# A dummy exponential first on ScalarE, the first load of x in two, and a new order of the work

## The chip, the cores and the metric

One core of a Trainium2 chip runs the kernel. Its engines are TensorE (PE in the profile; PEld are its weight loads), VectorE (DVE), ScalarE (ACT), GpSimd (POOL) and SyncE (SP); 16 DMA engines move data between HBM and SBUF. The metric is the device time of one execution in microseconds (us); lower is better. Beside it stands the span, from the first to the last instruction of the program as the profiler records it.

## The reference

A causal depthwise convolution of 7 taps, with one softmaxed set of taps for each of 8 heads of 24 columns, is followed by a token mixer without softmax. Batch 8, 4224 tokens, 192 columns, a hidden width of 64, all float32 outside.

```python
w = softmax(weight, axis=-1)                     # (8 heads, 7 taps)
x = sum over k of w[h, k] * x_pad[b, s + k, h]   # causal, zero-padded by 6
wq, wk = x @ w_q, x @ w_k                        # (B, S, 64)
W_tok = einsum('bsd,btd->bst', wq, wk) / sqrt(64)
mixed = einsum('bst,btd->bsd', W_tok, x)
out = maximum(mixed, 0) @ w_out
```

Since nothing non-linear stands between `W_tok` and `mixed`, the kernel never forms the 4224 x 4224 matrix. It forms the 192 x 192 gram matrix of a batch, G = x^T x, then M = w_k^T G / 8 (64 x 192), and mixed = wq M.

## The kernel before, in words

**Tiling.** A batch's 4224 tokens are cut into 35 chunks of 122 (`CW`), each loaded with the 6 tokens before it, so that a chunk fills 128 partitions. x comes from HBM as float32 and is cast to bf16 by the loading DMA into `XW`, which holds five batches (`NX`). Batch 0 is loaded in four groups of 9, 9, 9 and 8 chunks, the others in two of 18 and 17. Chunk 0, the full chunks and the last chunk of a batch are each a DMA of their own, all issued on POOL's queue.

**Stages of a batch**, with the names that the profile shows:

1. *Convolution* (`conv`, L352 to L354): for each pair of heads and each group, a product of a banded 128 x 128 matrix (`BAND`) with the chunks, into one or two of the eight PSUM banks; drained as bf16 to `Y` by ScalarE or VectorE (`y`, L671).
2. *Transposes* (`tr_lo`, `tr_hi`, L358 to L360 and L728), drained by VectorE to `YTL` and `YTH` (L698, L738).
3. *Gram* (L795), six chunks a time, one bank for all; then a turn of part of it, and the product M (drains `gsb`, `gt`, `msb`, `mbd`).
4. *wq* (L757, L761), drained to `WQT` (L778).
5. *Mix* of the batch before, in five blocks: `mix_lo` (L888) and `mix_hi` (L900, L908) form the mixed tokens, a relu drains them to `RT` (L925, L926), `fin` (L954) and `fin_other` (L972) multiply by `w_out`, drains go to `OUT` (L993), and SP issues the store (L1001). The last batch's stores are halved.

**The start.** SP loads `weight` to all partitions (L366). VectorE writes an identity's ones, zeroes the run-up tile `RUNUP` and other small tiles. POOL cuts `IDENT` out of the ones with `affine_select` (L403). TensorE multiplies zeros from `RUNUP` (the run-up, L378) while nothing else is there to do. From `IDENT` come `STEP`, its transpose `STEPT` (copied by ScalarE, L424), and the 0/1 masks `OTHER` and `OWN` (L428 to L436). The softmax runs in `WEX` (maximum L440, differences L446 and L452, exponential on ScalarE L461, sums, reciprocal, product L466 to L471), gives `TAPS` (L473), and sixteen small products per fill (L353 and L354, "taps,stept") spread the taps into PSUM, from where ScalarE and VectorE copy the bands (L511). The first convolution needs the band, one more run-up (`run_3`) and all DMAs of the first group.

**Order.** Each piece of work is an `Op` with a number in the order of its creation. `PLAN` lists all numbers in the order in which they are placed, with a letter for the engine (P: TensorE in its op's own array shape, F: TensorE in the full 128 x 128 shape, A: ScalarE, D: VectorE, G: POOL, S: SP; a small letter: one drain for two banks) and, for TensorE's first op of a group, its PSUM bank. An engine executes its ops strictly in that order, each after its semaphore waits. The estimated lengths in the code (`ns`, `tail`, `lands`) are not used when the kernel is built. `turns` fixes a minimal order of VectorE's first ops.

**Numbers used below.** In the order before: 14 `IDENT`'s select, 38 chunk 0 and 39 chunks 1 to 8 of the first group, 40 to 43 the other groups of batch 0, 57 to 60 batch 1, and so on. In the order after, one op more from number 23 on (the dummy) and two more from 42 on (the load's second part).

Of the kernel before, what the change touches and what calls it, by code (L numbers as in the profile page):

```python
# [14 lines left out]
39G 0S 2D 14G 1D 9D 5D 6D 7D 15D 20D 21D 4D 38G 40G 44S 41G 42G 43G 57G 58G 59G 60G 16P3 17P2 19A 23D 24D  # L15
25D 22D 26A 27D 28D 29D 30D 18P5 31P4 34P1 37P7 35D 36D 3D 32A 73P0 33A 75P3 10D 11D 76D 77P1 78A 79P7 80D
12D 74A 109P3 135P7 87P0 88A 61G 62G 110D 85F1 86A 83F6 84D 81F0 82A 93F4 94D 13D 89F6 90A 95F5 45S 96A 91F0
111F3 92A 112D 137P 136P 97F2 98D 103F5 104A 99F4 101F3 102D 8D 46S 113F0 114D 119P6 120D 100A 117F5 118D
115F4 116D 139P 121P2 122D 123P1 124D 138P 140P 141D 49A 47A 48A 125P6 126D 133P7 134A 127P3 154P1 155D 156A
51A 151F4 152A 153D 148F6 149A 150D 157F1 158A 159D 131P0 132D 129P5 130D 128A 50A 142F4 143A 176F7 177D  # L20
178F6 179D 202P4 169P0 170D 171D 163P2 54A 52A 53A 144P5 147A 146A 145A 160P6 204P 166P0 161A 162D 244P5
164D 165A 167A 168D 203P 230P6 247D 233A 56A 216P0 219A 180P1 181D 190P7 191D 186P5 187D 215P2 217A 55A 63G
184P6 185D 218D 282P0 182P7 206P 200P2 201D 183D 205P 188P5 189D 285P2 283A 284A 286D 287A 288P0 289A 290A
279P6 280D 281A 207P 194P5 195A 64G 294P2 295A 192P1 193A 208D 209P0 296D 229P6 210D 231D 232A 220P4 224P2
221P 222A 243P0 245A 246A 225P 226D 227D 258P6 261A 223D 228S 65G 66G 309P7 310D 198P4 199A 196P2 272P3 274A
67G 68G 69G 70G 71G 72G 105G 106G 107G 108G 172G 173G 174G 175G 303G 304G 234P0 238P5 271P4 273D 235P 236D
197A 237A 307F7 308D 239F 240D 241A 242S 211F4 213A 257P0 259D 212A 260A 214A 248P2 252P6 275P5 249P 250D
251A 253P 254A 276P 277D 278S 300P0 301A 347P4 291P2 292A 293A 297P5 298A 333P0 255D 256S 302D 413P1 414A
415A 350A 335P 306G 299D 315P3 316D 319P5 320D 346P6 348D 349A 311F1 312D 361F2 364A 419F3 420D 421A 425F6
426D 427A 305G 337P 317P2 321P1 322D 266P4 318D 262P6 313F3 314D 267F 268A 269D 263F 264D 265A 270S 422F1  # L30
423D 424A 375F3 378D 329P4 330A 331P5 332D 334P 416P6 417A 418D 410P1 411A 412D 325P4 326A 327P3 328A 360P6
362D 363A 355P1 351P4 356P 357D 358A 352P 402P6 404D 353D 354A 359S 323P3 324A 389P7 392A 369P1 365P5 370P
371A 372D 374P3 366P 367A 368D 373S 376A 436F7 428F1 429D 430A 431F5 432D 433A 437D 403P3 336P 338P 339D
442P6 443D 446P5 447D 434P2 435D 340P7 405A 377A 379P3 341A 388P0 390A 383P5 342F7 344A 343A 391D 345A 380F
381A 382D 384F 385A 386D 387S 440F0 441D 473P1 475A 476D 397P3 406P5 393P6 398P 399D 400A 407P 408A 409S
394F 543F0 544D 545D 395A 396A 401S 438F4 439D 488P5 555P2 556A 557A 491D 474P6 477A 448P0 444P7 537P1 538A
449D 460P4 445D 540P5 541A 542D 456P3 457A 454P1 455D 502P0 505A 463P 501P6 503D 504A 458P5 552P0 553A 554D
539D 450P3 451A 459A 464P 558P6 559A 560D 546P0 547A 548D 461P 452P5 453D 478P6 487P2 489A 490D 482P0 479F
480D 481A 563F5 564D 483F 484D 485A 486S 492P2 465P 530P7 532A 549F5 550D 551A 493F 494D 495A 561F7 562D
516F1 519A 496P5 515P2 517A 518A 529P0 531A 497P 498D 499D 500S 462P 571P1 572D 569F7 570D 670F2 671D 672D  # L40
466A 467F5 468A 533P4 510P0 506P6 565F5 566D 469F2 472A 471A 470A 534F 535D 536S 567F3 568D 511P 512A 513D
507P 508A 509A 514S 520P4 573P2 575P0 576D 521F 522A 523D 664F6 665A 643F3 646A 667F0 666A 673F4 585P6 586A
674A 574D 581P2 582A 675A 587P3 589P 577P7 578A 668D 669D 601P0 615P6 604D 524P1 600P4 602D 525P 526A 629P7
632D 527A 528S 603A 618D 590P 579P0 580A 583P2 592P 584A 609P4 628P6 630A 631D 605P0 610F 611A 612D 688F2
689D 606P 656P6 607A 608D 613S 614P4 616D 588P 657P7 617A 659A 591P 642P1 623P4 658A 619P6 644A 645A 593D
594F3 595D 624F 625A 626D 620F 621A 622D 627S 679F0 680A 681D 596F2 599A 598A 597A 690F4 691D 637P6 633P0
638F 639D 640A 685F2 686A 687D 676F4 677D 678A 634F 635D 636A 641S 682F6 683D 684A 651P2 647P4 660P1 652P
653D 654A 648P 661P 662D 663S 728P0 731A 742P7 745D 698P6 699D 700P3 701D 649A 650A 655S 702P2 703D 791P0
792A 793A 692P7 693D 797P5 798A 799D 800P3 756P0 759A 801D 794P1 795A 796A 694P5 695D 727P6 696P0 697D 802D
704P3 705D 729A 806P1 807D 808A 712P0 713D 710P6 711A 730A 817P5 818D 815P3 816D 708P1 709A 706P2 707A 732P6  # L50
741P4 743A 744D 736P0 733F 734A 735D 770F2 773A 737F 750P4 783P3 746P6 738A 739D 740S 751P 752A 753A 755P1
757A 758D 785D 747P 748A 714P0 716P 803P4 749A 754S 784P3 924P1 718P 804A 805D 812P6 813D 814D 933P4 934D
935A 786A 719P 717P 715P 720A 925D 926A 769P6 771D 772A 760P4 787P3 764P0 788P 789A 790S 761P 762A 763D 765P
721P2 766D 767A 768S 722A 809P6 810A 841P3 843P 723P5 725A 724A 726A 811D 823P7 824D 819P6 820D 829P2 921P0
830D 821P4 822D 918P5 919D 827P2 828D 825P7 826D 922A 923A 920A 927P0 928A 837P4 855P6 858D 842P 839P7 840D
869P5 872D 929A 838D 835P1 836A 831P0 832D 846P 778P6 774P1 854P4 856D 857A 779P 780A 781A 775P 776D 845P
883P0 886A 777D 782S 844P 847A 930P5 833P4 931A 932D 834A 848P2 849D 944P3 945D 863P0 868P6 859P4 870D 871A
897F2 900A 864F 865A 866D 860F 861A 862D 867S 942F3 943D 896P6 898A 910P2 912D 877P0 899A 873P4 878P 879A
880D 911P3 913A 874P 875D 876A 881S 882P6 884D 885A 850F2 853A 939F0 940D 941A 936F3 937A 938D 852A 851A
914P5 905P6 887P0 906P 907D 908A 891P3 915P 916A 917S 888P 892P 893D 946P2 947D 954P7 956P6 957D 952P5 953D  # L60
948P3 949D 955D 889A 890A 894A 895S 950P0 951D 968P4 982P1 985D 966P2 967A 996P5 999A 958P6 959A 962P7 963A
901P2 981P0 983D 984A 902P 1009P5 903D 904A 909S 1011A 1012D 973P 1010P7 1013A 971P 995P0 997D 998A 986P2
990P5 987P 988D 989A 1024F7 1027A 991P 992A 993D 994S 1004P0 1000P2 1005P 1006A 1007A 1023P6 1001P 1002A
1003D 1008S 1037P5 1039D 1025A 1026D 972P 969P 970P 974D 1038P2 1040A 960P0 961D 1018P5 1014P2 975F4 976D
# [11 lines left out]
class Op:  # L76


    n = 0
# [144 lines left out]
def bass_lightweight_conv__then__hypermixer_token_mlp_kernel(  # L224
# [31 lines left out]
    def groups_of(b):  # L256
        size = 9 if b == 0 else 18
        return [list(range(c, min(c + size, NCC))) for c in range(0, NCC, size)]
# [828 lines left out]
```

## Time and profile before

| | us |
|---|---|
| Runs, median (lowest to highest of 3) | 169.34 (169.01 to 169.45) |
| The profiled execution, its own time | 167.91 |
| Its span | 166.2 |
| First convolution begins | 7.59 |
| First / second / third / fourth group of batch 0 landed | 6.66 / 9.52 / 11.82 / 13.83 |
| First half of batches 1, 2, 5, 7 landed | 20.65 / 29.45 / 74.67 / 110.17 |
| Second half of batches 1, 2, 7 landed | 24.90 / 33.96 / 114.38 |
| Last product of TensorE ends | 160.27 |
| Last drain ends | 161.33 |
| Last store lands | 165.62 |

The landings are the times of issue plus the times to landing in the trace. A few of the page's groups, for the cost of a drain on either engine (line, engine, operation, tiles, count | busy us, mean ns of one | idle before):

```profile
L671 ACT CAST y<-ps 122x432 bf16<-122x432 f32 (+2 forms) x71 | 33.7, 519 | 10.9 <-PE ps L354 9.4
L993 DVE COPY out_sb<-ps 128x384 f32<-128x384 f32 (+1 forms) x64 | 32.9, 540 | 6.1 <-PE ps L972 4.6
L993 ACT COPY out_sb<-ps 128x384 f32<-128x384 f32 (+1 forms) x72 | 31.4, 479 | 8.8 <-PE ps L972 8.2
L671 DVE CAST y<-ps 122x408 bf16<-122x408 f32 (+2 forms) x57 | 31.6, 587 | 5.4 <-PE ps L354 3.1
```

The mean is an instruction's length from its own start; where two overlap, the busy time counts the overlap once.

### The profile page before, as it was taken

The numbers are of one execution on the slowest core, as the hardware profiler recorded it, in microseconds if no ns is written. First come the engines' busy times: TensorE is split into PE (matmuls) and PEld (weight loads), VectorE is DVE, ScalarE is ACT, GpSimd is POOL, SyncE is SP. The second block draws the span as 40 slices with busy tenths as digits, with TensorE's granted clock in tenths as the row PEclk, the third lists the DMA queues.
The fourth block names the chain that finished last, engine by engine and source line by source line (L and its number), as shares of the span: only waits on it lengthen the run. The fifth ranks groups of instructions, "written<-read, shape, count | busy, mean of one in ns | idle before, by whom it ended". The sixth has DMA issues, their size and how long they took to land.

```text
span 166.2 us, 6578 instructions
## 1 busy us (share of the span) xinstructions
PE 155.5 (94%) x2852; PEld 115.2 (69%) x2852; DVE 132.6 (80%) x276; ACT 117.3 (71%) x285; POOL 30.4 (18%) x39
## 2 busy tenths in 40 slices
PE   6969999999999999999999999998999999999940
PEld 2448758777777687787767777687888867785620
DVE  5566889879799799898967889966698889879960
ACT  1446186699958978868587788894856895969920
POOL 7999653535400200000000000000000000000000
PEclk9999999999999999999999999999999999999997
DMA  2999999999999999999999999999330595478996
GB/s 20 175 191 185 205 191 196 189 194 195 301 322 238 285 290 282 316 263 191 296 287 283 285 281 302 324 250 343 142 127 4 196 365 219 186 287 323 376 366 234
DMA packets 48156, 40.33 MB, mean 243 GB/s; under 512 B 37632, under 2 KB 40960, under 8 KB 48128
## 3 DMA queue, kind: packets, MB, share of 16 engines
q0 software_dynamic: 36128, 13.61, 68.6%
q1 hardware_dynamic: 12000, 26.31, 43.9%
q8 instruction: 22, 0.36, 0.8%
q14 instruction: 6, 0.05, 0.1%
HBM read 27.56 MB, written 25.95 MB: 322 GB/s over the span
## 4 chain that ended last, share of the span: by engine, by line
PE 79%; DMA 8%; POOL 4%; ACT 3%; issue 2%; DVE 0%; another core or an unknown queue 0%; DVEq 0%; POOLq 0%
PE ps L795 13%; PE ps L954 12%; PE ps L972 10%; DMA xw<-in_x_dram 8%; PE ps L353 6%; PE ps L888 5%; PE ps L757 5%; PE ps L358 4%; PE ps L352 4%; PE ps L728 4%; PE ps L761 4%; PE ps L908 3%; PE ps L359 3%; POOL xw L556 3%; PE ps L354 3%
## 5 line engine op out<-in xcount | busy, mean ns | idle before, releaser
L925 ACT ACTIVATE rt<-ps 128x512 bf16<-128x512 f32 (+1 forms) x70 | 37.6, 559 | 5.8 <-PE ps L888 3.7
L671 ACT CAST y<-ps 122x432 bf16<-122x432 f32 (+2 forms) x71 | 33.7, 519 | 10.9 <-PE ps L354 9.4
L993 DVE COPY out_sb<-ps 128x384 f32<-128x384 f32 (+1 forms) x64 | 32.9, 540 | 6.1 <-PE ps L972 4.6
L993 ACT COPY out_sb<-ps 128x384 f32<-128x384 f32 (+1 forms) x72 | 31.4, 479 | 8.8 <-PE ps L972 8.2
L671 DVE CAST y<-ps 122x408 bf16<-122x408 f32 (+2 forms) x57 | 31.6, 587 | 5.4 <-PE ps L354 3.1
L556 POOL DMA_DIRECT2D xw<-in_x_dram x34 | 29.9, 892 | 24.8 <-issue 17.4
L795 PEld LDWEIGHTS ps<-y 122*64 122x64 bf16 x840 | 29.0, 111 | 4.0 <-issue 1.2
L795 PE MATMUL ps<-y 122*64 122x64 bf16 (+2 forms) x840 | 31.6, 221 | 0.1
L926 DVE TENSOR_SCALAR rt<-ps 128x512 bf16<-128x512 f32 (+1 forms) x42 | 26.0, 628 | 6.9 <-PE ps L888 5.3
L698 DVE COPY ytl<-ps 128x976 bf16<-128x976 bf16 (+1 forms) x40 | 23.2, 588 | 3.5 <-PE ps L360 2.6
L972 PE MATMUL ps<-wol,rt 64*128 64x192 bf16 (+1 forms) x264 | 25.1, 248 | 0.2
L954 PE MATMUL ps<-woh,rt 64*128 64x192 bf16 x264 | 22.9, 248 | 0.7 <-ACT rt L925 0.4
L353 PE MATMUL ps<-xw,band 128*64 128x432 bf16 (+2 forms) x82 | 19.0, 332 | 0.6 <-DMA xw<-in_x_dram 0.6
L354 PE MATMUL ps<-xw,band 128*64 128x432 bf16 (+2 forms) x82 | 19.1, 334 | 0.0
L972 PEld LDWEIGHTS ps<-wol,rt 64*128 64x128 bf16 (+1 forms) x264 | 15.9, 114 | 4.4 <-PE ps L954 1.0
L778 ACT CAST wqt<-ps 128x512 bf16<-128x512 f32 (+1 forms) x26 | 13.6, 546 | 6.5 <-PE ps L761 6.3
L954 PEld LDWEIGHTS ps<-woh,rt 64*128 64x128 bf16 x264 | 12.5, 113 | 7.9 <-issue 1.4
L954 PE MATMUL ps<-wol,rt 64*128 64x192 bf16 x175 | 15.4, 243 | 0.0
L761 PE MATMUL ps<-yth,wqh 128*64 128x512 bf16 (+1 forms) x72 | 14.8, 361 | 0.0
L757 PE MATMUL ps<-ytl,wql 128*64 128x512 bf16 (+1 forms) x72 | 14.7, 367 | 0.0
L888 PE MATMUL ps<-wqt,msb 64*128 64x512 bf16 (+1 forms) x72 | 13.8, 363 | 0.0
L738 DVE COPY yth<-ps 128x732 bf16<-128x732 bf16 x24 | 12.1, 530 | 0.5 <-PE ps L728 0.5
(116 smaller groups left out, 207.4 us busy)
## 6 DMA issues: line engine op xcount, KB each, us to landing
out_dram<-out_sb SPq DMA_DIRECT2D x28, 768.0 KB, 7.2
xw<-in_x_dram POOLq DMA_DIRECT2D x7, 816.0 KB, 36.2
xw<-in_x_dram POOLq DMA_DIRECT2D x7, 768.0 KB, 38.6
out_dram<-out_sb SPq DMA_DIRECT2D x8, 384.0 KB, 3.9
xw<-in_x_dram POOLq DMA_DIRECT2D x2, 432.0 KB, 6.9
out_dram<-out_sb SPq DMA_DIRECT2D x8, 96.0 KB, 4.9
xw<-in_x_dram POOLq DMA_DIRECT2D x1, 384.0 KB, 5.1
xw<-in_x_dram POOLq DMA_DIRECT2D x8, 45.8 KB, 23.7
```

The source lines that it names most:

```text
L353: e.matmul(out[0:64], lhsT[:, 0:64], rhs, **k)
L354: return e.matmul(out[64:128], lhsT[:, 64:128], rhs, **k)
L556: lambda e, op, part=part: e.dma_start(*part),
L671: return e.copy(dst, src) if op.engine == "ACT" else e.tensor_copy(dst, src)
L698: lambda e, op: e.tensor_copy(YTL[:, b % NYT, t0:t1], bank(mm_l.bank).bitcast(BF16)[:, 0:cols]),
L757: last = e.matmul(ps[64 * i : 64 * i + DH, 0:n], WQL[:, :], YTL[:, b % NYT, starts[i] : starts[i] + n], start=True, stop=False)
L795: mm = e.matmul(bank(where.bank)[p : p + 64, o : o + z - r], Y[0:w, yb, c, r : r + 64], Y[0:w, yb, c, r:z], start=st, stop=end, skip_group ...
L925: return e.activation(dst, src(), AF.Relu)
L926: return e.tensor_scalar(dst, src(), 0.0, None, op0=ALU.max)
L954: last = e.matmul(bank(op.bank + a)[:, (i - q) * D : (i - q) * D + D], RT[p, slot, a if lo else 2, i:n:nt], WOL[p, :] if lo else WOH[p, :] ...
L972: last = e.matmul(bank(fh.bank + a)[:, (i - q) * D : (i - q) * D + D], RT[p, slot, a, i:n:nt], WOL[p, :], start=False, stop=True, skip_gro ...
L993: return e.copy(dst, src) if op.engine == "ACT" else e.tensor_copy(dst, src)
```

## The change

- ScalarE's first instruction becomes a dummy: `Exp` of one column of `RUNUP` into a new tile `EARLY`, which nobody reads. It needs the run-up tile alone; STEPT's copy comes after it.
- The main load of the first group (chunks 1 to 8) is split into chunks 1 to 3 and chunks 4 to 8. Only the first part may go before `IDENT`'s select.
- VectorE's minimal order puts the zeroing of `STEPT`, `WQH`, `WKT` and `WKB` before `STEP`, `OWN` before the maximum, and the zeroing of the last columns of `WQT` behind the second difference.
- The second run-up has 5 products instead of 6.
- Two estimates change (`tail`, `ident`'s length), which the built program doesn't contain.
- `PLAN` is another order: engines of drains, array shapes, banks and sequence. The first convolutions now stand as follows on TensorE: all four of the first group, three of the second, a gram, a transpose, the fourth of the second group; before it was the first group, a transpose, a gram, then the second group. ScalarE has 296 ops instead of 284, VectorE 265 instead of 276, POOL 36 instead of 35.

```diff
 PLAN = """
-39G 0S 2D 14G 1D 9D 5D 6D 7D 15D 20D 21D 4D 38G 40G 44S 41G 42G 43G 57G 58G 59G 60G 16P3 17P2 19A 23D 24D
-25D 22D 26A 27D 28D 29D 30D 18P5 31P4 34P1 37P7 35D 36D 3D 32A 73P0 33A 75P3 10D 11D 76D 77P1 78A 79P7 80D
+40G 2D 1D 9D 5D 6D 7D 4D 14G 41G 39G 42G 43G 44G 45G 59G 60G 61G 62G 63G 64G 23A 10D 11D 12D 15D 20D 21D 22D
+0S 24D 25D 26D 3D 27A 28D 16P6 17P3 18P2 29D 30D 31D 19A 32P0 35P2 33A 38P4 36D 37D 75F5 76D 34A 77P0 78A
...
-        size = 9 if b == 0 else 18
-        return [list(range(c, min(c + size, NCC))) for c in range(0, NCC, size)]
+        cuts = [0,9,18,27,NCC] if b == 0 else [0, 18, NCC]
+        return [list(range(c, z)) for c, z in zip(cuts, cuts[1:])]
...
+    EARLY = sbuf("early", [128, 1], F32)
...
-        tail=3500,
+        tail=3200,
...
-        1800,
+        1160,
...
-    run_2 = run_up(6, after=[turned])
+    run_2 = run_up(5, after=[turned])
...
+    early = add("ACT", lambda e, op: e.activation(EARLY[:, :], RUNUP[:, 0:1], AF.Exp), 1600, needs=[zero_r], vt=-9, kind="early")
+    stept.after.append(early)
...
-    turns = [one, zero_r, zero_x, eps, zero_e, zero_x0[0], step, by_tap, other, zero_s, mx, sub, mine, own, sm, rc, wn, taps, *bands[2:]]
-    turns += [zero_w, zero_q, *zero_k, zero_m, zero_x0[1]]
+    turns = [one, zero_r, zero_x, eps, zero_e, zero_x0[0], zero_s, zero_q, *zero_k, step, by_tap, other, own]
+    turns += [mx, sub, mine, zero_w, sm, rc, wn, taps, *bands[2:], zero_m, zero_x0[1]]
...
-        n = len(full)
-        parts.append(
-            (
-                XW[:, b % NX, full[0] : full[0] + n, :],
-                bass.AP(x_t, base + (CW * full[0] - KC + 1) * D, [[D, 128], [CW * D, n], [1, D]]),
-            )
-        )
+        for c, z in ((1, 4), (4, cs[-1] + 1)) if (b, gi) == (0, 0) else ((full[0], full[-1] + 1),):
+            parts.append(
+                (
+                    XW[:, b % NX, c:z, :],
+                    bass.AP(x_t, base + (CW * c - KC + 1) * D, [[D, 128], [CW * D, z - c], [1, D]]),
+                )
+            )
...
-            first = (b, gi) == (0, 0) and part[0].shape[1] > 1 and len(part[0].shape) == 3
+            first = (b, gi, k) == (0, 0, 1)
```

## The prediction

> **What bounds the kernel now.** I read the page's busy times first, then its row of DMA shares.
>
> ```profile
> PE 155.5 (94%) x2852; PEld 115.2 (69%) x2852; DVE 132.6 (80%) x276; ACT 117.3 (71%) x285; POOL 30.4 (18%) x39
> DMA  2999999999999999999999999999330595478996
> ```
>
> TensorE works 94% of the span. The 16 DMA engines are full from the second to the 28th of 40 slices, and again in the last ones. So three things can set a moment: TensorE's own work, a load of x that it waits for, and, at the end, the stores. The chain of waits says where the loads do (columns: start, length, what).
>
> ```profile
> 7.27 13.38 DMA xw<-in_x_dram
> 20.69 0.37 PE ps L353
> ...
> 113.87 0.51 another core or an unknown queue
> 114.42 0.36 PE ps L353
> ```
>
> The chain leaves TensorE twice for x: the first half of batch 1 lands at 20.65 (7.27 + 13.38) and TensorE starts on it at 20.69; the second half of batch 7 lands at 114.38 and TensorE, idle since 113.87, starts at 114.42. Everywhere else after 10 us it has work: 148.2 us busy in the 150 us from 10 to 160. Then the timeline of the start.
>
> ```profile
> 1.33 1.01 POOL L556 DMA_DIRECT2D xw<-in_x_dram  x1 [0.81 <-POOLq L1072]
> ...
> 2.77 0.20 DVE L412 COPY step<-ident 128x128 bf16<-128x128 bf16 x1 [0.57 <-POOL ident L403]
> ...
> 3.47 2.74 PE L378 MATMUL ps<-runup 128*128 128x512 bf16 x6
> 3.63 1.28 ACT L424 ACT_TABLE_LOAD   x1 [3.63 <-PE ps L360]
> ...
> 4.24 0.22 DVE L452 TENSOR_TENSOR wex<-wex,other 128x56 f32<-128x56 f32 x1
> ...
> 5.00 0.30 ACT L461 ACTIVATE wex<-wex 128x112 f32<-128x112 f32 x1
> ...
> 6.09 0.29 DVE L473 TENSOR_TENSOR taps<-own,wtap 128x128 bf16<-128x128 f32 x1
> ...
> 8.17 0.17 DVE L385 MEMSET wqt<- 64x128 uint32 x1
> ...
> 8.73 1.12 DVE L671 CAST y<-ps 122x432 bf16<-122x432 f32 x2
> ...
> 9.97 0.11 PEld L359 LDWEIGHTS ps<-ident,y 122*64 122x64 bf16 x1 [1.51 <-ACT y L671]
> ```
>
> ScalarE loads its table at 3.63, only when the first matrix to copy is there, so the softmax exponential starts at 5.00 although its operand is complete at 4.46 (4.24 + 0.22). The taps follow at 6.09. Later VectorE clears three small tiles (0.17 at 8.17, then two of 0.11) ahead of its first drains of y (8.73), and TensorE's transposes wait for those until 9.97, 1.5 us. Last, the DMA side: the issue of the load of chunks 9 to 17 (KB, us to landing) and three windows (length; busy us of PE, PEld, DVE, ACT, POOL; clock; DMA share; GB/s).
>
> ```profile
> xw<-in_x_dram POOLq DMA_DIRECT2D x1, 432.0 KB, 6.3
> ```
>
> ```profile
> 5.00:6.00 1.00, 1.00 (x3) 0.15 (x1) 0.60 (x3) 0.30 (x2) 1.00 (x2) 1.00 1.59 189
> 6.00:7.00 1.00, 0.77 (x26) 0.56 (x27) 0.35 (x2) 0.00 (x0) 1.00 (x3) 1.00 1.30 131
> ...
> 162.00:164.00 2.00, 0.00 (x0) 0.00 (x0) 0.00 (x0) 0.00 (x0) 0.00 (x0) 0.96 1.03 363
> ```
>
> That load is issued at 3.24 and lands at 9.52. The share falls to 1.30 between 6 and 7, where the first two loads are through and this one's rows come slowly: a bubble of about 0.3 us of full flow (131 GB/s against 188). In the last stretch the stores keep the engines at a share of 1.03, after TensorE has nothing left.
>
> **Part by part.** All against the profiled execution, 167.91 us with a span of 166.2; the runs have a median of 169.34 (169.01 to 169.45), 1.43 above it, so I subtract the same difference from both.
>
> *Dummy exponential.* It waits for the run-up tile alone (written by 1.34), so the table load of 1.28 is over at about 2.6 and the dummy itself (0.30, the row of the real one, at most) at 2.9; all that is queued behind it on ScalarE waits for later things. The real one then starts when its operand is there: 4.46 instead of 5.00, about 0.5 earlier. STEPT's copy goes behind it (0.18, over at about 5.0), hidden since its reader comes after the taps. The exponential, four VectorE steps and taps keep their lengths: taps end at 5.9 instead of 6.38. *One run-up less* is needed for that: six took 2.74 from 3.47, to 6.2; five (0.43 each) end at 5.8. With six the fills would wait 0.3. The fills then fall wholly into the time when TensorE still runs slowly (run-up matmuls of 512 columns take 0.43, later ones of 512 columns 0.22), some 0.2 more for the two. The first convolution so moves from 7.59 to 7.2 or 7.3.
>
> *Tiles zeroed elsewhere.* The clearing of STEPT, WQH and WKT/WKB (0.16 + 3 x 0.11 = 0.49) moves into VectorE's idle 0.57 before 2.77; OWN (0.38) ahead of the weight's landing at 3.72, where it just fits; WQT (0.17) into the wait for the exponential. VectorE's drains of the first y's come about 0.9 us earlier (0.5 from the taps, 0.4 from the clearing that stood before them).
>
> *Where that leads.* In the new order TensorE does not go on to these transposes: three convolutions of the second load stand ahead, and what is queued behind them (gram, transposes, VectorE's copies of these) waits with them. So its gap ends not at 9.97 but when that load lands, 9.52 + d, d being the shift of the loads. Convolution, gram and transpose fill the time to the third and fourth landing (11.82 + d, 13.83 + d). The fourth group's convolutions started at 14.80, with one gram of 0.50 done that the new order puts later: like for like 14.30 against 13.85 + d, a gain of 0.45 to 0.5 less d. At batch 1 the new order has a turn and, net, one more product for WQ ahead (0.34 + 0.44 in the chain for two half-sums of each kind, about 0.5 for one pair), which uses that up: TensorE arrives near 20.5 + d and waits no longer than now. So **0.48 - d**.
>
> *The load in two* costs one more issue on POOL. The rows are 0.59 for 122 rows, 1.01 for 1024, 1.00 for 1152: 384 and 640 rows cost about 0.7 and 0.85. The first part ends at 2.1 instead of 2.34, IDENT's select follows 0.25 earlier, then 640 rows, chunk 0 (0.57), and the second group is issued at 3.85, not 3.24: 0.6 later, and every later load with it. How much of it reaches the landings, the trace doesn't show. Lower bound: the first rows flow 0.3 earlier as the first issue is shorter, and the bubble closes: d = -0.3. Upper: the second group's rows come 3.0 us after its issue as now, and everything behind is 0.6 later. Between, as the queue holds two loads ahead while they wait: **d = 0.2**. So -0.28, from -0.78 to +0.12.
>
> *The order.* Both orders hold 470 turns of TensorE with 101 and 104 changes between its array shapes, too little to price. I compared what stands ahead of the first use of each load. For the last (second half of batch 7) the new order has three grams (0.50 each), a MIX_LO and a convolution (0.3 to 0.4 each) more ahead, 2.1 us. TensorE arrives near 115.7, after the landing at 114.38, and the wait of 0.51 goes: **-0.5** (0 if order costs it elsewhere). For the others the difference is within 1.7 us and the present slack holds, the tightest being batch 5 (landed 74.67, used 75.57).
>
> *VectorE to ScalarE.* ScalarE has 296 turns for 284, VectorE 265 for 276. By the page, a drain of y is 0.475 on ScalarE (33.7 / 71) and 0.554 on VectorE (31.6 / 57), one of out_sb 0.436 and 0.514, a relu 0.537 and 0.619. Seven y and eight out_sb go over, four relus come back: 0.55 + 0.62 - 0.33 = 0.85 less in all, 0.4 per engine. TensorE hides half or more of it: **-0.2**, from -0.85 to the loss of the ScalarE rival.
>
> *The tail.* From the store issued at 150.33 to the end the queue stays full: 4.9 MB at about 370 GB/s, 13 us, to 164.4. So the end hangs on when this store goes out, not on TensorE's last product. In the new order two FIN groups of the last batch (eight products 0.33; with four, half) stand before it: **+0.33**, from 0 to 0.5. The last drains are four in a row on ScalarE (1.74), against two on VectorE (1.02) now; they hide behind the stores by some 0.5, and without that cover cost 0.7.
>
> Sum: -0.28 - 0.5 - 0.2 + 0.33 = **-0.65**: 167.26 for the profiled execution, **168.7** for the runs.
>
> **Rivals.** *The feed is late by more.* The four clearings now run while POOL writes the 640 rows' descriptors. If they hold it up by their full 0.49, d is 0.6 + 0.49 = 1.1 and the sum +0.25: 169.6. Against it: the first issue ran beside a clearing of 0.46 (VectorE at 1.50) and took 1.01, no more than 1.00 later without one. [...] The row just given speaks against it for this clearing, so I give this rival little.
>
> *ScalarE becomes the bound* (the slower side). Between the turns of the sixth and seventh gram (94.6 and 117.9) ScalarE now has 44 drains and is busy 18.9 of 23.3 us, 9.04 of 10 from 100 to 110; the new order gives it 49 there, 2.4 us more at 0.48. If its idle time there can't be used, TensorE's banks come free late, by 2.4 at most; with half, and without the relief, -0.65 + 0.2 + 1.2: 170.1. From 0.45 lost upwards the kernel is slower than now. For it: VectorE, at 9.68 in the same 10 us, can't help. Against: 4.4 us of idle.
>
> *The drains gain in full.* With 0.85 taken and d = -0.3 the sum is -1.8: 167.5 to 168.1.
>
> *The table load doesn't move, or comes twice*: then the start stays, 1.28 more in the second case, most of it hidden by the wait for the second load; -0.65 + 0.28: 169.0. The single load now serves copy and exponential, so this is unlikely.
>
> **Chances.** Below 0.3% (0.51 us) a measurement here can't be told from no change. Forecast 0.50, spread 168.2 to 169.2 (0.35 faster, 0.15 same); late feed 0.12 (same 0.09, slower 0.03); ScalarE 0.20 (slower); full gain 0.15 (faster); table 0.03 (same). Faster 0.50, same 0.27, slower 0.23. The range, 167.6 to 170.2, leaves out the outer parts of the ScalarE and full-gain cases.
>
> **What would show it.** Table load near 1.4, exponential near 4.5, taps over by 5.9: right at the start. The second group's landing gives d. No wait on the load at 114 and a first use after 115: the second term. A store run of 13 us that starts later against TensorE's work: the tail. It is wrong if the waits move to drains on ScalarE between 95 and 118, or if the loads land over 0.7 later.

## The result and the profile after

| | before | after |
|---|---|---|
| Runs taken together, median (lowest to highest) | 169.39 (169.01 to 169.82), 4 runs | 171.3 (171.15 to 172.24), 4 runs |
| Ratio, 95% interval | | 1.0131 (1.0085 to 1.0177) |
| Profiled execution, its own time | 167.91 | 171.15 |
| Its span | 166.2 | 169.4 |
| Weight landed / real exponential begins | 3.72 / 5.00 | 4.22 / 4.99 |
| First convolution begins | 7.59 | 7.93 |
| Groups 1 to 4 of batch 0 landed | 6.66 / 9.52 / 11.82 / 13.83 | 7.89 / 11.82 / 14.10 / 16.13 |
| First / second half of batch 1 landed | 20.65 / 24.90 | 22.41 / 26.93 |
| Last product of TensorE ends | 160.27 | 162.85 |
| From there to the end of the span | 5.88 | 6.57 |

The change makes the kernel 1.3% slower, some 2.2 us by the ratio (1.9 by the medians). First the page of after: the busy times, and two rows of 40 slices.

```profile
PE 154.7 (91%) x2803; PEld 116.7 (69%) x2811; DVE 127.4 (75%) x265; ACT 122.6 (72%) x297; POOL 31.1 (18%) x40
...
PEclk9996999999999999999999999999999999999996
DMA  3999999999999999999999999998250585478996
```

TensorE is busy 0.8 us less than before while the span is 3.2 us longer: the time went into idling, not into more work. PEclk falls to 6 in the fourth slice (12.7 to 16.9 us), where before it was full. The chain of waits (start, length, what) leaves TensorE early and once more:

```profile
0.70 0.62 issue
1.32 0.89 POOL xw L560
2.61 1.41 POOL xw L560 x2
4.02 7.80 DMA xw<-in_x_dram
...
33.80 0.86 issue
```

From the start to 11.82 nothing but loads of x stands on the chain: the issues on POOL, then 7.80 us from the second group's issue to its landing. The pieces at 20.69 and 114.42, where the chain of before waited for batches 1 and 7, are gone. New is an "issue" of 0.86, in which TensorE waits for nothing that the profile shows. The timeline of the start:

```profile
0.80 1.28 ACT L441 ACT_TABLE_LOAD   x1 [0.80 <-PEq L1076]
...
1.32 0.89 POOL L560 DMA_DIRECT2D xw<-in_x_dram  x1 [0.81 <-POOLq L1076]
...
2.10 0.20 ACT L441 ACTIVATE early<-runup 128x1 f32<-128x1 bf16 x1
...
2.54 11.56 POOL L560 DMA_DIRECT2D xw<-in_x_dram  x13
...
4.24 0.21 DVE L444 TENSOR_REDUCE wmx<-wt_f 128x8 f32<-128x56 f32 x1 [0.72 <-DMA wt_f<-in_weight_dram]
...
4.74 0.22 DVE L456 TENSOR_TENSOR wex<-wex,other 128x56 f32<-128x56 f32 x1
...
4.99 0.30 ACT L465 ACTIVATE wex<-wex 128x112 f32<-128x112 f32 x1 [2.69 <-DVE wex L456]
...
6.07 0.29 DVE L477 TENSOR_TENSOR taps<-own,wtap 128x128 bf16<-128x128 f32 x1
...
7.93 0.36 PE L353 MATMUL ps<-xw,band 128*128 128x216 bf16 x2 [0.50 <-DMA xw<-in_x_dram]
...
11.87 0.28 PE L354 MATMUL ps<-xw,band 128*64 128x216 bf16 x1 [2.67 <-DMA xw<-in_x_dram]
```

The table load stands at 0.80, even ahead of the dummy's wait for the run-up tile, and the dummy is through at 2.30. But VectorE's first step on the weight waits for it until 4.24, so that the real exponential begins at 4.99 as before. The first convolution waits 0.50 for x, and then TensorE idles 2.67 us, to 11.87, for the second group. That group's issue (KB, us to landing; the latter was 6.3), and windows (length; busy us of PE, PEld, DVE, ACT, POOL; clock; DMA share; GB/s):

```profile
xw<-in_x_dram POOLq DMA_DIRECT2D x1, 432.0 KB, 7.8
```

```profile
4.00:5.00 1.00, 1.00 (x4) 0.32 (x3) 0.65 (x3) 0.01 (x1) 1.00 (x2) 1.00 0.77 69
5.00:6.00 1.00, 0.78 (x2) 0.00 (x0) 0.78 (x4) 0.35 (x2) 1.00 (x2) 1.00 1.11 115
6.00:7.00 1.00, 0.58 (x32) 0.58 (x32) 0.33 (x2) 0.10 (x1) 1.00 (x2) 1.00 1.41 164
7.00:8.00 1.00, 0.50 (x10) 0.17 (x4) 0.75 (x2) 0.55 (x2) 1.00 (x3) 1.00 1.05 103
8.00:9.00 1.00, 1.00 (x12) 0.44 (x12) 0.61 (x1) 0.36 (x1) 1.00 (x2) 1.00 1.07 123
12.00:14.00 2.00, 2.00 (x46) 2.00 (x44) 0.61 (x1) 0.94 (x2) 2.00 (x2) 0.66 1.59 191
14.00:16.00 2.00, 2.00 (x17) 1.55 (x13) 1.70 (x3) 0.15 (x1) 2.00 (x4) 0.50 1.57 187
165.00:167.00 2.00, 0.00 (x0) 0.00 (x0) 0.00 (x0) 0.00 (x0) 0.00 (x0) 0.81 1.03 372
```

From 4 to 9 us the DMA engines move 69 to 164 GB/s, where the kernel before had 182 to 189, and 131 from 6 to 7. From 12 on they are full again (191). Behind the idle 2.67 us TensorE's clock is at half (0.50 from 14 to 16). In the last row the stores run at 372 GB/s with TensorE through, as before.

### The profile page after: what moved, and what is told of

Read it like the earlier page. It is cut to its first block, busy times and chain, and to the rows that moved or that the text cites. A ratio compares the mean times of both kernels' runs of the same rounds, so it can differ in the third digit from the quotient of the medians.

```text
span 169.4 us, 6485 instructions
## 1 busy us (share of the span) xinstructions
PE 154.7 (91%) x2803; PEld 116.7 (69%) x2811; DVE 127.4 (75%) x265; ACT 122.6 (72%) x297; POOL 31.1 (18%) x40
## 4 chain that ended last, share of the span: by engine, by line
PE 81%; ACT 6%; DMA 5%; issue 2%; POOL 2%; ACTq 0%; POOLq 0%
PE ps L799 15%; PE ps L958 11%; PE ps L976 10%; PE ps L354 7%; PE ps L359 5%; PE ps L353 5%; PE ps L892 5%; PE ps L732 5%; DMA xw<-in_x_dram 5%; PE ps L761 4%; PE ps L765 4%; PE ps L912 4%; PE ps L360 3%; ACT out_sb L997 3%; PE ps L355 2%
## 5 line engine op out<-in xcount | busy, mean ns | idle before, releaser
L675 ACT CAST y<-ps 122x432 bf16<-122x432 f32 (+2 forms) x78 | 36.8, 525 | 16.0 <-PE ps L355 9.7
L997 ACT COPY out_sb<-ps 128x384 f32<-128x384 f32 (+1 forms) x80 | 34.5, 477 | 7.4 <-PE ps L976 6.9
L929 ACT ACTIVATE rt<-ps 128x512 bf16<-128x512 f32 (+2 forms) x66 | 34.5, 556 | 6.3 <-PE ps L892 4.5
L997 DVE COPY out_sb<-ps 128x384 f32<-128x384 f32 (+1 forms) x56 | 28.7, 537 | 10.3 <-PE ps L976 9.8
L675 DVE CAST y<-ps 122x432 bf16<-122x432 f32 (+2 forms) x50 | 28.0, 587 | 6.3 <-PE ps L355 4.5
L799 PEld LDWEIGHTS ps<-y 122*64 122x64 bf16 (+1 forms) x840 | 29.0, 111 | 4.0 <-issue 1.5
L799 PE MATMUL ps<-y 122*64 122x64 bf16 (+4 forms) x840 | 31.7, 222 | 0.0
L930 DVE TENSOR_SCALAR rt<-ps 128x512 bf16<-128x512 f32 (+2 forms) x46 | 28.0, 630 | 4.4 <-PE ps L892 3.3
L354 PE MATMUL ps<-xw,band 128*64 128x432 bf16 (+2 forms) x92 | 21.4, 334 | 2.7 <-DMA xw<-in_x_dram 2.7
L355 PE MATMUL ps<-xw,band 128*64 128x432 bf16 (+2 forms) x92 | 21.4, 334 | 0.0
L958 PE MATMUL ps<-wol,rt 64*128 64x192 bf16 x146 | 12.9, 243 | 0.0
```

The costliest lines, as they stand in the source:

```text
L354: e.matmul(out[0:64], lhsT[:, 0:64], rhs, **k)
L355: return e.matmul(out[64:128], lhsT[:, 64:128], rhs, **k)
L675: return e.copy(dst, src) if op.engine == "ACT" else e.tensor_copy(dst, src)
L799: mm = e.matmul(bank(where.bank)[p : p + 64, o : o + z - r], Y[0:w, yb, c, r : r + 64], Y[0:w, yb, c, r:z], start=st, stop=end, skip_group ...
L929: return e.activation(dst, src(), AF.Relu)
L930: return e.tensor_scalar(dst, src(), 0.0, None, op0=ALU.max)
```

## The experiments

All ratios are against the kernel before on the same chip; in brackets the 95% interval. "Halt" is idle time of TensorE that the profile calls "issue". A ratio rests on many executions, a trace shows one of them.

### One part put back, one part alone

**e1**: the changed kernel with the first load in one (one op less, so the plan's numbers above 40 fall by one).

```diff
-for c, z in ((1, 4), (4, cs[-1] + 1)) if (b, gi) == (0, 0) else ((full[0], full[-1] + 1),):
+for c, z in ((full[0], full[-1] + 1),):
```

> The kernel after with the first load in one again (chunks 1 to 8), all else kept. Theory S (the load in two makes the queue of x run dry, and it restarts slowly): the second group lands at 9.3 to 9.9 us instead of 11.82, TensorE waits under 0.7 us for it instead of 2.7, its clock no longer falls between 12 and 16 us, and the time is 168.5 to 169.5. Theory V (VectorE's clearing of small tiles holds up POOL's descriptors): it still lands after 11 us and the time stays at 171. Theory O (the new order itself is slower): landing at 9.5, time over 170.5.

Measured: 1.0058 (1.0028 to 1.0089). The second group lands at 9.56, the exponential begins at 4.47, the first convolution at 7.14, with no half clock. So the load in two costs more than half, and 0.6% stays with the load in one.

**e2**: the kernel before with the load in two and nothing else (the second part's issue, `40G`, behind `IDENT`'s select, `14G`).

```diff
-39G 0S 2D 14G 1D
+39G 0S 2D 14G 40G 1D
```

> The kernel before with the first load in two, the second part issued behind the identity's select, and nothing else. Theory S: the second group lands at 11.3 to 12.0 us; the old order does a gram and a transpose (0.9 us) ahead of it, so TensorE waits 1 to 1.5 us and the time is 170 to 171. Theory V: the tiles are cleared at the old times, so it lands 0.6 later at most, at 10.1, and the time is 169.2 to 169.9. Theory O: as V.

Measured: 1.0114 (1.0069 to 1.0158), second group landed at 11.84. The split alone makes the kernel slower, in the order of before too.

**e3**: the kernel before with the dummy alone.

```diff
-16P3 17P2 19A 23D
+16P3 17P2 23A 19A 24D
```

> The kernel before with the dummy exponential alone. All theories: table load in the first 2.2 us, the real exponential at 4.5 us, taps over at 5.9, second group landed at 9.5 as before. The forecast's reasoning gives TensorE's transposes of the first group 0.3 to 0.5 earlier, and a time of 168.9 to 169.4, since the wait for batch 1 at 20.65 takes most of that back. If the weight lands 0.5 later in this kernel too, as it does in the kernel after (4.22 instead of 3.72), the taps stay at 6.4 and the time at 169.4.

Measured: 1.0008 (0.9987 to 1.0028). The exponential begins at 4.48 and the taps at 5.57, 0.5 earlier, as the prediction had it, and nothing comes of it: TensorE waits 1.30 us for its transposes to 9.68 (before also 1.30, to 10.00) and 0.29 to 20.57 for batch 1.

### VectorE's clearing

**e4**: the changed kernel with STEPT, OWN, WQT, WQH, WKT and WKB zeroed or written where they were before.

```diff
-turns = [one, zero_r, zero_x, eps, zero_e, zero_x0[0], zero_s, zero_q, *zero_k, step, by_tap, other, own]
-turns += [mx, sub, mine, zero_w, sm, rc, wn, taps, *bands[2:], zero_m, zero_x0[1]]
+turns = [one, zero_r, zero_x, eps, zero_e, zero_x0[0], step, by_tap, other, zero_s, mx, sub, mine, own, sm, rc, wn, taps, *bands[2:]]
+turns += [zero_w, zero_q, *zero_k, zero_m, zero_x0[1]]
```

> The kernel after with STEPT, WQH, WKT, WKB, WQT cleared and OWN formed at the old places of VectorE's order, load in two kept. Theory V: the second group lands at 9.5 to 10.2 us, time 169 to 169.7. Theory S: it lands at 11.5 to 12.1, time 171 to 171.8 (a little more than after, since y's first drains come 0.4 later). Theory O: time over 170.5, landing open.

Measured: 1.0192 (1.0152 to 1.0232), second group landed at 11.96. Without the four clearings beside POOL's issues the load comes no sooner; they are not what holds it up. The time is no shorter either.

### Two guesses at the front of the order

**e5**: e1 with a cast of `w_out` (57A) moved behind the next drain on ScalarE, since in e1 TensorE waits 0.69 us at 21.19 for a copy of the gram that is queued behind that cast.

```diff
-56A ... 57A
+56A 57A
```

> The new order with the first load in one (as in the first experiment) and the cast of the upper part of W_out moved on ScalarE from ahead of the first gram's drain to behind the next cast of W_out. Theory G (the drain sits behind a cast that waits for W_out's landing at 20.1 us, so TensorE waits 0.7 us at the turn, 21.2): that wait goes, the turn starts at 20.6 or earlier, and the time is 0.4 to 0.8 us under the 1.0058 of the first experiment, so 1.001 to 1.003 of before. Rival (what is left lies in the order further on): the wait goes and the time stays at 1.005 or more.

Measured: 1.0063 (1.0033 to 1.0092). The wait is gone and the time stays. In this execution the second group landed at 10.44 and TensorE's clock was at half from 10.9 to 14.3.

**e6**: the changed kernel with the first gram and a transpose ahead of the second group's convolutions.

```diff
-83P1 89P5 90D 87P4 88A 137P0 111P3
+137P0 111P3 83P1 89P5 90D 87P4 88A
```

> The kernel after, load in two kept, with the first gram and the first transpose ahead of the second group's convolutions, as in the order before. Theory K (a good part of the loss comes from TensorE lying idle from 9.2 to 11.9 us, after which its clock is half until 16.0): no half clock after 7 us, TensorE as far at 16 us as before plus 0.9 of work done in the gap, and the time 1.5 to 2.5 us lower than after, near 1.003 of before or 169.3. Rival (the late landings alone set it): the second half of batch 1's landings stay 2 us late, and the time falls by less than 0.7 us.

Measured: 1.0128 (1.009 to 1.0165), the same as the changed kernel. In the profiled execution (171.16 us, mean granted clock 0.989) the clock stays full from 5.4 us on, but the one idle time of 2.67 becomes three of 0.71 to 1.26 between 9.2 and 14.2: TensorE has no more x than in the changed kernel, in whatever order it takes the rest. The other three executions had a mean clock of 0.969 to 0.971 and took 170.62 to 170.90.

### Other ways of splitting

**e7**: the kernel before, split into chunks 1 to 7 and chunk 8. **e8**: split as in the change, but both parts issued ahead of `IDENT`'s select.

```diff
-((1, 4), (4, cs[-1] + 1))
+((1, 8), (8, cs[-1] + 1))
```

```diff
-39G 0S 2D 14G 40G
+39G 0S 2D 40G 14G
```

> The kernel before with the load in two as chunks 1 to 7 and chunk 8 instead of 1 to 3 and 4 to 8. Theory D (the queue of x runs dry when the first part is short; a restart is slow): 896 rows keep it fed to 5.5 us, so the second group lands at 9.5 to 10.2 us and the time is within 0.3% of before. Theory N (each DMA more at the start costs the stream the same, whatever its size): it lands at 11.5 us or later, and the time is 1.008 to 1.014 of before.

> The kernel before with the load in two (chunks 1 to 3 and 4 to 8), both parts issued before the identity's select. Theory D: the second part is issued 0.3 us earlier than with the select between, the dry time is shorter, and the second group lands at 10.8 to 11.6 us; the softmax comes 0.8 later (select at 3.1), first convolution near 8.3; time 1.006 to 1.015 of before. Theory I (it is the select between the two issues that holds up the descriptors): it lands at 9.5 to 10 us. Theory N: it lands at 11.8.

Measured: e7 1.0026 (0.9996 to 1.0056), second group at 11.80; e8 1.0023 (1.0001 to 1.0045), second group at 11.19. Both splits bring the late landing: moving the cut leaves it at 11.80, and without the select between the parts it is still 1.67 later than before. In each, the expectation that had the landing right had the time too high. What the landing costs in the end differs more than it does itself (0.2% in e7 and e8, 1.1% in e2).

### The order taken apart

**e9**: dummy, zeroing and run-up as in the change, load in one, the order of before. **e10**: the first 289 turns (to the third store, about 43 us) in the new order, the rest as before. **e11**: the other way round. **e12**: e9 with the load in two. No code but the plan differs between e1, e9, e10 and e11:

```diff
 PLAN of e10 = [turns of the new order that are among the first 289 of e9] + [the rest, in the order of before]
 PLAN of e11 = [the first 289 of e9, in the order of before] + [the rest, in the new order]
```

> The changed kernel with the load in one piece and with the order of before; the dummy exponential, the other places of the zeroing and five run-up matmuls stay. Theory O (the rest of what the changed kernel loses with the load in one, 0.6%, is the new order's): a ratio of 0.998 to 1.002, taps starting at 5.4 to 5.6, the second group landing at 9.5. Theory P (the dummy, the zeroing and the shorter run-up cost it together): 1.004 to 1.008, and a gap on TensorE in the first 20 us that the kernel before doesn't have.

> As the kernel with the order of before, but its first 289 turns (to the third store or so, some 43 us) stand in the new order; everything behind stands as before. Theory F (the front of the new order costs the 0.6%: second group's convolutions first, a halt of TensorE at 32 to 35 us): 1.005 to 1.009, the stores after 45 us later by 0.7 to 1.3 us and by a constant. Theory R (the rest of the order costs it, its tail of stores above all): 0.998 to 1.002 and stores as before.

> The other half: the first 289 turns as before, the rest in the new order. Theory R: 1.003 to 1.007, no halt of TensorE of 0.8 us at 32 to 35, the time from the last product of TensorE to the end 0.3 to 0.5 us longer than before's 5.9. Theory F: 0.996 to 1.002. If the two halves cost a part each, each is about 1.003.

> All of the change but the order: dummy, zeroing, run-up and the load in two, in the order of before. If the load in two costs the same in each order, the one-load kernel's ratio and 0.7% more (1.0131 less 1.0058): 1.005 to 1.010. If the order of before takes the late second group in its stride (the three groups of e7 and e8 did, at 1.0026 and 1.0023): 1.000 to 1.004. The second group lands at 11.2 to 12.0 in both cases.

| | front | rest | load | ratio (95%) |
|---|---|---|---|---|
| e9 | before | before | one | 0.9999 (0.9979 to 1.0020) |
| e11 | before | new | one | 0.9993 (0.9966 to 1.0020) |
| e10 | new | before | one | 1.0096 (1.0059 to 1.0133) |
| e1 | new | new | one | 1.0058 (1.0028 to 1.0089) |
| e12 | before | before | two | 1.0068 (1.0042 to 1.0093) |
| after | new | new | two | 1.0131 (1.0085 to 1.0177) |

So the change comes apart: dummy, zeroing and run-up cost nothing, the order behind 43 us nothing, the order ahead of it 0.6% (e1) to 1.0% (e10). In e10 TensorE also waits 0.50 us at the joint of the two orders, to 43.52, for a copy on VectorE, so the 0.6% is the better figure. The load in two costs 0.7% with either order when the rest of the change is there (0.69 and 0.73 points, uncertain by 0.3 and 0.6), and 0.2% to 1.1% in the kernel before (e2, e7, e8). In e9 two waits of TensorE show where the earlier start goes:

```profile
8.86 0.24 PE L359 MATMUL ps<-ident,y 122*64 122x122 bf16 x1 [0.85 <-ACT y L674]
...
12.18 0.92 PE L352 MATMUL ps<-xw,band 128*128 128x216 bf16 x8 [0.95 <-DMA xw<-in_x_dram]
```

Its first convolution begins at 6.96, 0.63 earlier than before, and its transposes start at 8.86 instead of 10.00. Then it stands 0.95 us until the third group has landed (12.13). An earlier start didn't help TensorE, since it then lacked x.

### The halt at 32 us

Every kernel with the new front halts for 0.82 to 0.88 us between 32 and 35 us (after, e1, e4, e5, e6, e10), amid a row of transposes of one turn, which has one wait, at its head. In e1:

```profile
31.26 0.22 PE L359 MATMUL ps<-ident,y 122*64 122x122 bf16 x1
31.26 0.27 PE L360 MATMUL ps<-ident,y 122*64 122x122 bf16 x2
32.35 0.24 PE L359 MATMUL ps<-ident,y 122*64 122x122 bf16 x1 [0.82 <-issue]
```

By the trace's records, 960 to 962 of TensorE's instructions (products, weight loads and some 17 others) stand ahead of the halt in each of these kernels, and 2498 ahead of one of 0.81 in e3: the difference is 6 times 256. The DMA queues show what comes in such blocks (window of 1 us in after; packets, MB, share):

```profile
q0 software_dynamic: 478, 0.18, 151.6%
q8 instruction: 1, 0.02, 5.8%
```

One packet of 16 KB on an instruction queue, 22 in the whole run, which is 63 bytes for each of the 5721 instructions that the trace has of TensorE. That fits 64 bytes for each, 256 to a packet (an estimate from the two counts; that the packets are TensorE's instructions is part of it). **e13** (from e1) and **e14** (from after) cut the ten run-up products into thirty narrower ones of as many columns in all, 40 more instructions, products and loads, ahead of everything else.

```diff
-run_1 = run_up(4, needs=[zero_r])
+run_1 = run_up([160] * 12 + [128], needs=[zero_r])
...
-run_2 = run_up(5, after=[turned])
+run_2 = run_up([176] * 10 + [160] * 5, after=[turned])
...
-run_3 = run_up(1, after=fills)
+run_3 = run_up([256] * 2, after=fills)
```

> The changed kernel with the load in one piece, and its ten run-up matmuls cut into thirty narrower ones with the same columns in all: 40 more PE instructions ahead of everything else. Theory I (TensorE fetches its instructions in blocks of 256, a block has to last some 5.3 us while loads of x fill the DMA engines, and the block that ends at instruction 960 lasts 4.5 us in the new order): the same place in the program now lies in another block, which lasts 5.3 us, so the halt at 32 us is gone or under 0.3 us, and the ratio goes from 1.0058 to 0.999 to 1.003. Rival (the halt belongs to the transposes, or to a wait that isn't shown): a halt of 0.8 us stays behind the same transposes, ratio 1.004 to 1.008.

> The changed kernel as it is, with the load in two, and the same 40 instructions more. Theory I: the halt at 34.7 us is gone, the ratio goes from 1.0131 to 1.006 to 1.009, which is what the load in two costs alone (e12: 1.0068). Rival: 1.011 to 1.015 and the halt stays.

Measured: e13 1.0049 (1.0021 to 1.0076), e14 1.0158 (1.0131 to 1.0185), above both ranges; e14 has a halt of 0.86, to 34.76, too. The halt in e13:

```profile
30.75 0.33 PE L731 MATMUL ps<-ident,y 122*64 122x122 bf16 x5
31.93 0.35 PE L731 MATMUL ps<-ident,y 122*64 122x122 bf16 x6 [0.86 <-issue]
```

Place: it has left the transposes of L359 and L360 and stands 40 instructions earlier in the program, in those of L731, again behind 961 instructions. So it goes by the count of instructions, as blocks of 256 would have it, and not by a wait of the kernel. Size: it is no shorter, against the expectation that a block that lasts 5.3 us (e1's 4.5 and its halt of 0.82, an estimate) would be in time. The block lasted 5.4 here, but its packet came 3.9 us after TensorE entered the block ahead (3.1 in e1). In all twelve kernels that halt at this edge TensorE goes on 2.2 to 2.6 us after the packet (after: 32.39 and 34.66). The kernel before reaches the edge 2.2 us after it (28.71 and 30.89) and goes on at 2.6 (31.29), with an idle time of only 0.15. What the halt costs in the end is open: no run took it away, e3 has one of 0.81, to 73.63, at a ratio of 1.0008, and in e1's profiled execution TensorE's last product ends only 0.20 us later than in the kernel before, the halt included.

**e17** and **e18** cut the front once more, at the first convolutions of batch 1 (142 turns, about 22 us).

```diff
 PLAN of e17 = [the first 142 of e9, in the order of before] + [the rest, in the new order]
 PLAN of e18 = [the same 142, in the new order] + [the rest, in the order of before]
```

> As the kernel with the load in one and the order of before (e9: 0.9999), but from turn 142 on (behind the first convolutions of batch 1, some 22 us) in the new order. Theory I (the halt at the block of instructions costs it): the halt of 0.8 us after some 960 PE instructions is there and the ratio is 1.003 to 1.008. Rival (the first 22 us cost it, where TensorE waits for the second group): 0.998 to 1.002.

> The other half: the first 142 turns in the new order, everything behind as before. Theory I: no halt of 0.8 us at 32 us, 0.998 to 1.002. Rival: 1.003 to 1.008, with the loss seen before 22 us.

Measured: e17 1.0172 (1.0131 to 1.0213), e18 1.0043 (1.0011 to 1.0074). e17 tells nothing on its question: at the joint TensorE waits 0.87 and 0.71 us (to 25.94 and 27.0), which neither whole order does. e18 goes against the halt as the only cause: its executions together lose 0.4%, while the one that was profiled has the halt (0.46), and a wait of 1.96 us for the second group to 10.13, and took 168.07, less than the median of before (168.43).

```profile
10.13 0.28 PE L353 MATMUL ps<-xw,band 128*64 128x216 bf16 x1 [1.96 <-DMA xw<-in_x_dram]
...
31.74 0.24 PE L360 MATMUL ps<-ident,y 122*64 122x122 bf16 x1 [0.46 <-issue]
```

What sets e18's executions apart is the clock: five with a mean granted clock of 0.986 to 0.993 took 168.07 to 168.98, five with 0.976 to 0.982 took 169.42 to 170.57. All kernels with the new front and the load in one (e1, e5, e10, e13, e18) have executions of both kinds. Of the 46 executions that their ratios rest on, 28 had a clock of 0.983 or less, against 1 of 116 of the kernel before, run beside them, and 1 of 57 with the front of before (e3, e9, e11, e15, e16). These 28 took 1.0085 times the median of before in the mean, the other 18 1.0034 times. A stretch of half clock of 3.4 us, as e5's trace has it behind a wait of 1.83 for the second group, would lower the mean over 168 us by 0.01 (an estimate: half of 3.4 in 168).

The front's loss thus lies mostly in executions with a lower clock. Whether the half clock costs them the time or the wait for x ahead of it does, no run separates, and the halt's share of the rest stays open.

### Why the second group lands late

**e15**: the kernel before with a clearing of 0.54 us on POOL ahead of the second group's issue. **e16**: the kernel before with chunk 0's load in two, one transfer more, the large load whole.

```diff
-lambda e, op, part=part: e.dma_start(*part),
+lambda e, op, part=part, late=(b, gi, k) == (0, 1, 0): (e.memset(SPARE[:, :], 0.0) if late else None, e.dma_start(*part))[1],
```

```diff
-parts.append((XW[KC - 1 : 128, b % NX, 0, :], bass.AP(x_t, base, [[D, CW], [1, D]])))
+for r, z in ((0, 64), (64, CW)) if b == 0 else ((0, CW),):
+    parts.append((XW[KC - 1 + r : KC - 1 + z, b % NX, 0, :], bass.AP(x_t, base + r * D, [[D, z - r], [1, D]])))
```

> The kernel before with one clearing of a spare tile (128 x 512) on GpSimd ahead of the issue of the second group of x; no load is added. Theory T (the time of the issue decides): with an issue some 0.5 to 0.9 us later the second group lands at 11 to 12 and the ratio is 1.003 to 1.010. Theory N (the number of transfers decides): it lands later by no more than the issue, at 9.9 to 10.5, ratio 0.999 to 1.003.

> The kernel before with the load of chunk 0 in two (64 and 58 rows) and the load of chunks 1 to 8 in one: one transfer more ahead of the second group, another one than in the change. Theory N: the second group lands at 11.2 to 12, ratio 1.002 to 1.011. If only the split of the large load does it: 9.5 to 10.2 and 0.999 to 1.003.

Measured: e15 0.9983 (0.9962 to 1.0003), e16 0.9997 (0.9983 to 1.001). The second group is issued at 3.70 and 3.75 and lands at 9.62 and 9.61, nearly as in the kernel before (3.24 and 9.52). So neither an issue later by 0.5 nor one more transfer delays it; the split of the large load does. (With the split the issue is 0.66 to 0.80 later; no run has one so late with the load whole.) Where the delay lies is seen in the 16 completions that the trace has of the second group, as many as there are DMA engines (that each is one engine's is an estimate from that count). In us, from the trace's semaphore events (first, tenth, last):

```
before   9.00   9.21   9.52
e15      9.01   9.32   9.62
e16      9.00   9.23   9.61
e9       8.83   9.15   9.84
e5       8.87   9.19  10.44
e7       9.27   9.48  11.80   (15 of them by 9.92)
e8       9.30   9.73  11.19
e2       9.42  10.02  11.84
after    9.52  10.38  11.82
e12      9.51  11.39  12.31
```

The first completion comes at 8.8 to 9.5 everywhere. With the large load whole, the 16 come within 0.5 to 0.7 us where VectorE clears its tiles as before (before, e3, e15, e16), and within 0.6 to 1.6 us in the eight kernels where it clears them earlier; with the load split, in all eight, they are 1.9 to 2.8 us apart. TensorE goes on behind the last of them: in after it stands until 11.87, though ten had come by 10.38 and the last came at 11.82. Why a second part behind a first one of the same shape sets them apart, no run here shows.

## Why the prediction was wrong

The median is 2.6 us above the forecast and 1.1 above the range; a gain of 0.65 was forecast, a loss of 2.2 came (by the ratio; 1.9 by the medians).

**The step that failed: "Between, as the queue holds two loads ahead while they wait: d = 0.2."** The shift of the landings measured 2.3 us (11.82 against 9.52), beyond the bounds of -0.3 and 0.6 and beyond the 0.7 that the prediction itself named as a sign of being wrong. The bounds came from the issue on POOL (0.6 later; 0.78 measured) and from the mean flow (a bubble of 0.3), as if the 16 completions came as one. e15 shows that an issue 0.46 later is worth 0.10 at the landing, e16 that an added transfer with its 0.51 is worth 0.09. In after the first of the 16 completions is 0.5 later (9.52 against 9.00) and the last follows it after 2.3 instead of 0.5: most of the shift is this spread, which no row of the page shows. Of the shift, 0.7% or 1.2 us reach the time (e12; after against e1), and less in e7 and e8. With d = 2.3 the prediction's own sum would give 170.8, near the measured 171.3, but that is luck: it counts the whole shift, and gains that didn't come.

**"Too little to price"**, said of the order: its front costs 0.6% to 1.0% (e1, e10), with the load in one. The prediction compared what stands ahead of each load, and saw neither of the two places found: a TensorE that waits directly for a landing which, with the load in one, came anywhere between 9.52 and 10.44, with a lower clock in 28 of 46 executions, and a halt behind some 960 instructions (0.82 in e1, 0.86 in e10).

**The start, "0.48".** Where the weight landed on time, the exponential began at 4.47 (e1, e9) as forecast. In after the weight landed at 4.22; in all seven kernels with the load cut at chunk 3 it came at 3.90 to 4.22, in those without at 3.69 to 3.72, but for e10 (4.33). And the 0.48 had no worth even where it came: e3 and e9 lie within 0.2% of no change. TensorE's gap ended earlier, and the next one, for x, took it up. The table load was hoisted further than forecast (0.80, not 1.4).

**Batch 7, -0.5.** The wait at 114.38 is gone, as forecast, also with the load in one (e1, e11). It brought nothing that can be told: the rest of the order, with this term, most of the drains' -0.2 and the tail's +0.33, is at -0.07%, interval -0.34% to +0.20%; the forecast's -0.37 us would be -0.22%. **The tail** is 0.69 longer in after and 0.99 in e11, against 0.33 forecast; but it is 0.54 longer in e9 too, which ends in the order of before.

**The rivals.** "The feed is late by more" was the right place, at twice the size and for another reason: it put the delay on VectorE's clearings. e4 took the clearings away and the landing stayed at 11.96, so such a hold isn't what makes the 2.3. A small one is not excluded: with the load in one the second group lands at 9.52 to 9.62 in the four kernels with the clearings of before and at 9.56 to 10.44, 9.98 in the mean, in the eight with the new ones, 0.4 later, which is about the 0.49 of the clearings; but these eight differ in the dummy and the run-up too, and no run moves the clearings alone. "ScalarE becomes the bound" didn't come: between 35 and 153 us TensorE has no idle time over 0.2 us in after, and e11, which has most of the new drains, isn't slower. The table load neither stayed nor came twice.

## What to carry to other kernels

Here the load's last completion, not its mean flow, set when TensorE went on, and the split alone moved it by 2.3 us (e2: 11.84 against 9.52) where an issue 0.46 later moved it by 0.10 (e15): a change to the first loads can cost far more than the later issue that one computes; try the new cut alone and look at the spread of the completions, not only at the flow. A profile shows one execution: set its clock and time beside those of the others before explaining the median by it. Ahead of a stage that waits for data, an earlier start was worth nothing here (0.63 earlier in e9, ratio 0.9999): price it only up to the next landing. And an "issue" wait can go by the count of instructions, whatever the program does there, as in e13 (0.86, again behind 961 instructions, in other transposes): shift the program by some instructions and see whether it moves.

## What the runs showed of the hardware

- TensorE halted behind 960 to 962 instructions in the kernels with the new front (0.82 to 0.88 us; 0.46 in e18) and behind 2498 in e3 (0.81), 6 times 256 further on. After has 22 packets of 16 KB on an instruction queue, 256 instructions each by the estimate above. In the twelve kernels with the halt at the first of these edges TensorE went on 2.2 to 2.6 us after the block's packet. While x loaded, the packet came 2.8 to 4.4 us after TensorE entered the block ahead in the kernel before; behind the last loads (from 125 us on) 0 to 1.6.
- An idle time of 2.67 us was followed by half the clock from 12.6 to 16.0, one of 1.83 (e5) by half from 10.9 to 14.3, one of 2.89 (e14) by half for 6.8 us, and in e12 one of 1.59, to 12.35, with 0.93 more to 14.63, by half from 14.6 to 18.0, while one of 1.96 (e18) left it full. Three of the four stretches are 3.4 us long, the fourth twice that; what sets their start, no run here shows.
- With the load in two, a lower clock shows no cost: e6's execution at a mean clock of 0.989 took 171.16 us, its three at 0.969 to 0.971 took 170.62 to 170.90. With the new front and the load in one, the executions at 0.983 or less were 0.5% longer than the others.
